# Top-k attention and a leaky-ReLU MLP on one core: other banks for the MLP's block products, later evictions in its small chunks, and four units fewer on the short path

## The chip, the cores and the metric

The kernel runs on one core of one Trainium2 chip. The metric is the device time of the whole program in microseconds; lower is better. TensorE is called PE, VectorE DVE, ScalarE ACT, GpSimd POOL and SyncE SP, as in the profile. Each of these engines works through its own queue in the order in which the program was written out, and engines wait for one another through semaphores.

## The reference

```python
# q, k, v: (8, 8, 576, 64) float32
scores = scale * np.matmul(q, k.transpose(0, 1, 3, 2))
kth = np.partition(scores, -32, axis=-1)[..., -32:-31]
scores = np.where(scores >= kth, scores, -1000000000.0)
attn = np.exp(scores - np.max(scores, axis=-1, keepdims=True))
attn = attn / (np.sum(attn, axis=-1, keepdims=True) + 1e-09)
o = np.matmul(attn, v)
x = o.transpose(0, 2, 1, 3).reshape(4608, 512)
h = x @ w_in                      # (512, 2048)
out = np.maximum(0.01 * h, h) @ w_out   # (2048, 512)
```

Each row of scores keeps its 32 largest values, the rest are set to nothing, and after the softmax and the product with `v` every token goes through a two-layer MLP.

## The kernel before, in words

**Attention in units.** Two heads form a pair; a unit is 128 rows of queries of one pair against all 576 keys, two score rows of 576 per partition. There are 144 units (32 pairs, 4.5 blocks of 128 rows each; the half blocks of two pairs share a unit). The program is a loop of steps in twos, `even(s)` and `odd(s + 1)`. In step s, DVE runs `top_k` for unit s (`cur`): it makes pairs of maxima and minima (L308), then four rounds of the eight largest (`MAX8`, L314) with replacement in between (L319). Unit s-1 (`old`) is masked and exponentiated on ACT (L329 `nleast`, L335, L338, and L343, which writes `ze`), with a bias from two small POOL instructions (L330, L331). DVE takes the reciprocal of `ze` (L347, `rz`) and ACT normalizes (L350).

In `even(s)` DVE's queue holds most of unit s's rounds, then the reciprocal for unit s-1, and only then the last round. So DVE stands still in the middle of an even step when the `ze` of unit s-1 is late. The reciprocal for unit s-2 stands after the `pairs` instructions of an even step.

**Two ways to transposed weights.** The normalized weights have to be transposed before they are multiplied with `v`. Most units go the long way: POOL splits them into 16-bit halves (`split`, L359), SP stores these to DRAM (L360) and fetches them with a DMA transpose into `wT` (L364). The units in `HASTY` go the short way: nine transposes on PE (`transpose_in_haste`, L374) and two copies on ACT (`keep_transposed`, L380). `values_at(n)` says in which step unit n's values are weighed on PE (L403, L415): two steps after the unit's odd partner if hasty, otherwise three. ACT copies the result to `x` (L426).

**The MLP in chunks.** The tokens form two small chunks of 128 tokens and 17 chunks of 256. A chunk becomes ready when the last of its values has been weighed (`attended`). The MLP is a generator that yields after every few matmuls and says how many columns it used; each step calls `mlp_steps(budget)` in seven slots, between the attention's instructions. While the small chunks are in work, the budget of one slot is `EARLY_SHARE` = 500 columns; pieces are run as long as the running debt `owed` is above zero. Afterwards `slot_budget` spreads what is left up to the next chunk.

A small chunk computes its hidden layer in four groups of 512 columns (`hidden_of_few`, L439), each evicted with the leaky ReLU by ACT (L444), turned by PE (`turned`, L455) and copied to `gT` (L456). Then 16 matmuls of 512 columns make the output (`plain`, L623), which ACT copies in two halves (L633) and sends out from its own DMA queue (L634). All these ACT instructions are issued right after the matmuls that they wait for.

A big chunk computes its hidden layer in eight groups (L536, evicted at L524) and then seven products of 256 columns (L550), since sums of blocks, made on POOL (L475), stand in for an eighth. The products live in two PSUM tiles of one bank each, `pa` and `pb`, both halved. Their evictions (`keep_sum`, L558) are put on a list, `due`, which `catch_up()` empties: it is called after every fourth matmul of a product, before the normalizing in each step, and at other set places. So an eviction of a big chunk comes into ACT's queue a little after the matmuls that it reads. Step 7 puts six sums of weights on POOL's list (`sum_weights`), which `sum_now` works off two or three at a time.

All of `mlp`'s PSUM tiles (`ph`, `pt`, `pz`) share two buffers of the pool `ps_ml`.

Of the kernel before, what the change touches and what calls it, by code (L numbers as in the profile page):

```python
# [9 lines left out]
F32 = mybir.dt.float32  # L10
# [3 lines left out]
AF = mybir.ActivationFunctionType  # L14
# [6 lines left out]
def kernel(  # L21
# [13 lines left out]
    nc = tc.nc  # L35
    NPAIR, P, S = qT.shape
# [4 lines left out]
    SLOPE = 0.01  # L41
# [21 lines left out]
    work = ctx.enter_context(tc.tile_pool(name="work", bufs=2))  # L63
    small = ctx.enter_context(tc.tile_pool(name="small", bufs=5))
    halves = ctx.enter_context(tc.tile_pool(name="halves", bufs=3, space=bass.MemoryType.DRAM))
    kept = ctx.enter_context(tc.tile_pool(name="kept", bufs=1, space=bass.MemoryType.DRAM))
# [16 lines left out]
    gT = const.tile([P, NFC, CHMAX], F32, name="gT")  # L83
# [122 lines left out]
    for b in range(B):  # L206
        first = b % 2 == 1
# [225 lines left out]
    def hidden_of_few(ch, x):  # L433

        g_of = {}
        for j in range(NFC // 4):
            ph = ps_ml.tile([P, 512], F32, name="ph", tag="ml")
            for c in range(HP):
                nc.tensor.matmul(ph, x[:, c, 0:P], w_in[c][:, j * 512:(j + 1) * 512],  # L439
                                 start=(c == 0), stop=(c == HP - 1))  # L440
                if c == 1:
                    yield 2 * 512
            g_of[j] = raws.tile([P, 2 * DMODEL], U16, name="scale", bufs=2).bitcast(F32)
            nc.scalar.activation(g_of[j], ph, AF.Prelu, alpha=SLOPE)  # L444
            yield 2 * 512
            if j:
                yield from turned(j - 1, g_of)
        few[ch] = g_of
# [3 lines left out]
    def turned(j, g_of):  # L452
        pt = ps_ml.tile([P, 4, P], F32, name="pt", tag="ml")
        for i in range(4):
            nc.tensor.transpose(pt[:, i, :], g_of[j][:, i * P:(i + 1) * P], ident)  # L455
        nc.scalar.copy(gT[:, 4 * j:4 * (j + 1), 0:P], pt)  # L456
        yield 2 * P

    HALF, COLS = NFC // 2, DMODEL // 2
    summed = {}  # L460

    def w_at(f, j):
        return w_out[f // 4][:, f % 4, j * COLS:(j + 1) * COLS]
# [38 lines left out]
    due = []  # L502

    def catch_up():
        while due:
            due.pop(0)()

    def mlp(ch):

        n = CHUNKS[ch]  # L510
        t0 = sum(CHUNKS[:ch])
        x = x_of[ch]
        if ch < EARLY:
            yield from plain(ch, n, t0, x)
            return
        if ch == EARLY:
            sum_last_weights()
        halves_of_g = gT.rearrange("p (h f) n -> p h f n", h=2)
        (g11, g21), (g12, g22) = [[halves_of_g[:, h, :, r * P:(r + 1) * P] for r in range(2)] for h in range(2)]
        s1 = raws.tile([P, HALF, P], F32, name="top", bufs=2)  # L520
        s2 = raws.tile([P, HALF, P], F32, name="top", bufs=2)

        def keep_hidden(f0, ph):
            nc.scalar.activation(halves_of_g[:, :, f0, :], ph, AF.Prelu, alpha=SLOPE)  # L524
            if f0 % 4 == 3:
                at = slice(f0 - 3, f0 + 1)
                sum_later(s1[:, at, :], g21[:, at, :], g22[:, at, :], ALU.add, name="s1")
                sum_later(s2[:, at, :], s1[:, at, :], g11[:, at, :], ALU.subtract, name="s2")
                sum_later(g21[:, at, :], g11[:, at, :], g21[:, at, :], ALU.subtract, name="g21")

        for f0 in range(HALF):
            ph = ps_ml.tile([P, 2, CHMAX], F32, name="ph", tag="ml")
            for i in range(2):
                f = f0 + i * HALF
                for c in range(HP):
                    nc.tensor.matmul(  # L536
                        ph[:, i, 0:n], w_in[c][:, f * P:(f + 1) * P], x[:, c, 0:n],
                        start=(c == 0), stop=(c == HP - 1),
                    )
                    if c == 1:  # L540
                        yield 2 * n
                if i == 0:
                    catch_up()
                    yield 2 * n
            due.append(lambda f0=f0, ph=ph: keep_hidden(f0, ph))
            yield 2 * n

        def product(to, g, w, first=False):
            for f in range(HALF):
                nc.tensor.matmul(to, g[:, f, :], w(f), start=(first and f == 0), stop=(f == HALF - 1),  # L550
                                 skip_group_check=not first)
                if f % 4 == 3:
                    catch_up()
                    yield 4 * COLS

        def keep_sum(ps):
            part = work.tile([P, COLS], F32, name="o_sb", bufs=6)
            nc.scalar.copy(part, ps)  # L558
            return part

        def place(r, j):
            return out[t0 + r * P:t0 + (r + 1) * P, j * COLS:(j + 1) * COLS]

        def of(name):
            return lambda f: summed[name][:, f, :]

        pa = ps_ml.tile([P, 512], F32, name="pz", tag="ml")
        px = pa[:, 0:COLS]
        kept_sums = {}

        def kept(name, ps, then=None):
            def keep():
                kept_sums[name] = keep_sum(ps)
                if then is not None:
                    then()
            due.append(keep)

        def add(to, other, r, j):
            part = kept_sums[to]
            sum_later(part, part, kept_sums[other], ALU.add, (place(r, j), part))  # L580

        def sum_g12():
            for f0 in (0, 4):
                at = slice(f0, f0 + 4)
                sum_later(g12[:, at, :], g12[:, at, :], s2[:, at, :], ALU.subtract, name="g12")

        yield from product(px, g11, lambda f: w_at(f, 0), first=True)
        kept("p1", px)
        pb = ps_ml.tile([P, 512], F32, name="pz", tag="ml")
        py, pd = pb[:, 0:COLS], pb[:, COLS:2 * COLS]  # L590
        pz = py
        yield from product(py, g12, lambda f: w_at(f + HALF, 0), first=True)
        sum_g12()
        kept("p2", py, lambda: add("p1", "p2", 0, 0))
        yield from product(pd, g22, of("t4"), first=True)
        kept("p4", pd)
        need("s1")
        yield from product(pz, s1, of("t1"), first=True)
        kept("p5", pz)
        need("s2")  # L600
        yield from product(px, s2, of("t2"))
        kept("u2", px)
        need("g12")
        yield from product(pz, g12, lambda f: w_at(f + HALF, 1))
        kept("p35", pz, lambda: add("u2", "p35", 0, 1))
        need("g21")
        yield from product(px, g21, lambda f: w_at(f, 1))

        def finish():
            add("p4", "u3", 1, 0)  # L610
            add("p5", "u3", 1, 1)

        kept("u3", px, finish)
        yield 0
        catch_up()
        yield 0

    def plain(ch, n, t0, x):
        yield from hidden_of_few(ch, x)
        for r0 in range(0, n, P):  # L620
            pz = ps_ml.tile([P, 512], F32, name="pz", tag="ml")
            for f in range(NFC):
                nc.tensor.matmul(  # L623
                    pz[:, 0:DMODEL], gT[:, f, r0:r0 + P], w_out[f // 4][:, f % 4, :],
                    start=(f == 0), stop=(f == NFC - 1),
                )
                if f % 2 and f + 1 < NFC:
                    yield 2 * DMODEL
                if f == 7 and ch in few:
                    yield from turned(NFC // 4 - 1, few[ch])  # L630
            for j in range(2):
                o_sb = work.tile([P, COLS], F32, name="o_sb", bufs=6)
                nc.scalar.copy(o_sb, pz[:, j * COLS:(j + 1) * COLS])  # L633
                nc.scalar.dma_start(out[t0 + r0:t0 + r0 + P, j * COLS:(j + 1) * COLS], o_sb)  # L634
            yield 2 * DMODEL

    def mlp_cost(ch):
        n = CHUNKS[ch]
# [21 lines left out]

    HASTY = (*range(8), 14, 15, 142, 143)

    def values_at(n):

# [24 lines left out]
    def slot_budget(s):  # L691

        after = [at for at, _ in ready_at if at > s]
        if len(after) >= len(CHUNKS) - EARLY:
            return EARLY_SHARE
        until = after[0] if after else s + 1
        group = [GROUP * (at % 2 == 0 and at < len(steps)) for at in range(s, until)]
        return max((backlog[0] + sum(group)) / len(group) - group[0], 0.0) / SLOTS

    EARLY_SHARE = 500  # L700
# [3 lines left out]
    with tc.manual_schedule():  # L704
# [45 lines left out]
        for n in range(len(jobs) + 1):  # L750
            if n == len(jobs) - 1:
                first = first_scores(steps[0])
# [34 lines left out]
        def keep(weighed):  # L787
            for u, po in weighed:
                keep_values(u.pairs[0], po, u.b, u.q0)
# [171 lines left out]
```

## Time and profile before

| what | value |
|---|---|
| median of 3 runs | 1468.41 us (1467.25 to 1469.81) |
| the profiled execution | 1467.3 us, span 1465.5 us, granted clock 0.978 |
| DVE busy | 1319.9 us, 90% of the span |
| PE busy | 1366.7 us, 93% |
| ACT busy | 1040.4 us, 71% |
| POOL busy | 703.3 us, 48% |
| DVE waiting for `ze` (L343) | 51.3 us, 9 times |
| PE waiting for L558's evictions of products | 18.0 us, 25 times |

All times inside the profile count from the start of the span. A row of a timeline gives the start, the length, the engine and line, the operation with what it writes and reads, and in brackets how long the engine had been idle before it and who ended that. A row of the waits gives the total in us, how often, and the longest. The second part of the page cuts the span into 40 slices of 36.6 us, with one digit for the busy tenths of each.

### The profile page before, as it was taken

The numbers are of one execution on the slowest core, as the hardware profiler recorded it, in microseconds if no ns is written. First come the engines' busy times: TensorE is split into PE (matmuls) and PEld (weight loads), VectorE is DVE, ScalarE is ACT, GpSimd is POOL, SyncE is SP. The second block draws the span as 40 slices with busy tenths as digits, with TensorE's granted clock in tenths as the row PEclk, the third lists the DMA queues.
The fourth block names the chain that finished last, engine by engine and source line by source line (L and its number), as shares of the span: only waits on it lengthen the run. The fifth ranks groups of instructions, "written<-read, shape, count | busy, mean of one in ns | idle before, by whom it ended". The sixth has DMA issues, their size and how long they took to land.

```text
span 1465.5 us, 27960 instructions
## 1 busy us (share of the span) xinstructions
PE 1366.7 (93%) x9868; PEld 1068.4 (73%) x9868; DVE 1319.9 (90%) x3401; ACT 1040.4 (71%) x2159; POOL 703.3 (48%) x788
## 2 busy tenths in 40 slices
PE   7878886989999999999999999999999999999998
PEld 2344444767887878887878887888778888878787
DVE  7986789899999999999999999999999999999600
ACT  8785677677677777777777777767677777777521
POOL 3202432554646464656564545464655555555412
PEclk9967998999999999999999999999999999999999
DMA  8950044475676546675766656665766555664400
GB/s 324 339 185 33 1 126 125 110 202 169 178 181 185 153 130 185 193 190 130 201 165 185 170 138 185 196 179 153 194 179 164 145 154 138 166 144 137 117 12 15
DMA packets 379197, 229.83 MB, mean 157 GB/s; under 512 B 316208, under 2 KB 326960, under 8 KB 377136
## 3 DMA queue, kind: packets, MB, share of 16 engines
q1 hardware_dynamic: 378480, 227.52, 55.9%
q8 instruction: 77, 1.26, 0.4%
q14 instruction: 64, 0.52, 0.1%
q10 hardware_dynamic: 576, 0.52, 0.1%
HBM read 55.77 MB, written 94.37 MB: 102 GB/s over the span
## 4 chain that ended last, share of the span: by engine, by line
DVE 69%; PE 16%; issue 7%; ACT 4%; DMA 2%; POOL 1%; ACTq 0%; DVEq 0%; POOLq 0%; SPq 0%
DVE tops L314 33%; DVE pairs L319 26%; DVE pairs L308 7%; PE ph L536 6%; PE pz L550 4%; PE wide L403 2%; DMA raw<-in_weights_dram 1%; PE pz L623 1%; PE ph L439 1%; ACT s_sb L338 1%; DVE rz L347 1%; ACT s_sb L350 1%; ACT s_sb L335 1%; ACT s_sb L244 1%; DVE w_in L156 1%
## 5 line engine op out<-in xcount | busy, mean ns | idle before, releaser
L314 DVE MAX8 tops<-pairs 128x8 f32<-128x288 f32 (+1 forms) x1152 | 636.6, 593 | 0.0
L536 PE MATMUL ph<-x,w_in 128*128 128x256 f32 x2176 | 484.1, 382 | 4.2 <-ACT gT L524 4.2
L536 PEld LDWEIGHTS ph<-x,w_in 128*128 128x128 f32 x2176 | 408.8, 190 | 84.9 <-issue 16.0
L319 DVE MATCH_REPLACE8 pairs<-tops,pairs 128x288 f32<-128x288 f32 (+1 forms) x864 | 460.9, 539 | 0.0
L359 POOL COPY split<-s_sb 128x1152 uint16<-128x1152 uint16 x264 | 294.1, 1142 | 222.3 <-ACT s_sb L350 222.3
L350 ACT ACTIVATE s_sb<-s_sb,rz 128x576 f32<-128x576 f32 x288 | 206.8, 766 | 113.5 <-DVE rz L347 113.1
L330 POOL TENSOR_TENSOR nbias<-tops 128x2 f32<-128x2 f32 x144 | 73.1, 507 | 424.2 <-DVE tops L314 404.6
L550 PE MATMUL pz<-w_out,gT 128*128 128x256 f32 x1088 | 241.3, 379 | 1.7 <-ACT gT L524 1.7
L550 PEld LDWEIGHTS pz<-w_out,gT 128*128 128x128 f32 x1088 | 206.4, 190 | 31.1 <-ACT gT L524 2.5
L308 DVE TENSOR_TENSOR pairs<-s_sb 128x576 f32<-128x576 f32 x288 | 216.4, 791 | 9.9 <-ACT nleast L329 0.5
L338 ACT ACTIVATE s_sb<-s_sb,nbias 128x576 f32<-128x576 f32 x288 | 223.2, 781 | 0.8 <-POOL nbias L331 0.8
L335 ACT ACTIVATE s_sb<-s_sb,nleast 128x576 f32<-128x576 f32 x288 | 207.7, 768 | 4.8
L403 PE MATMUL wide<-wT,vt 128*64 128x128 f32 (+1 forms) x2560 | 157.4, 287 | 16.2 <-ACT wT L380 13.7
L403 PEld LDWEIGHTS wide<-wT,vt 128*64 128x64 f32 (+1 forms) x2560 | 129.9, 140 | 49.3 <-issue 30.4
L550 PE MATMUL pz<-raw,top 128*128 128x256 f32 x544 | 125.9, 384 | 8.4 <-ACT o_sb L558 5.7
L524 ACT ACTIVATE gT<-ph 128x512 f32<-128x512 f32 x136 | 80.6, 593 | 64.3 <-PE ph L536 64.2
L550 PEld LDWEIGHTS pz<-raw,top 128*128 128x128 f32 x544 | 100.9, 190 | 32.8 <-issue 13.0
L558 ACT COPY o_sb<-pz 128x256 f32<-128x256 f32 x119 | 44.6, 375 | 102.9 <-PE pz L550 93.6
L235 PE MATMUL wide<-kt,qt 64*64 64x352 f32 x1040 | 104.6, 474 | 0.0
L244 ACT COPY s_sb<-wide 128x704 f32<-128x704 f32 x130 | 99.4, 764 | 0.3 <-PE wide L235 0.3
L331 POOL TENSOR_SCALAR nbias<-nbias 128x2 f32<-128x2 f32 x144 | 84.0, 583 | 12.6
L550 PE MATMUL pz<-raw,gT 128*128 128x256 f32 x272 | 66.0, 385 | 12.9 <-ACT o_sb L558 12.3
(81 smaller groups left out, 1202.5 us busy)
## 6 DMA issues: line engine op xcount, KB each, us to landing
apart<-split SPq DMA_DIRECT2D x264, 288.0 KB, 2.3
raw<-in_weights_dram SPq DMA_DIRECT2D x15, 1024.0 KB, 7.0
vt<-in_vk_dram SPq DMA_DIRECT2D x32, 320.0 KB, 3.8
qt<-in_qT_dram SPq DMA_DIRECT2D x32, 288.0 KB, 3.7
kt<-in_kT_dram SPq DMA_DIRECT2D x32, 288.0 KB, 3.7
out_dram<-o_sb SPq DMA_DIRECT2D x68, 128.0 KB, 2.2
kept<-gT SPq DMA_DIRECT2D x12, 576.0 KB, 3.8
s_sb<-kept SPq DMA_DIRECT2D x12, 576.0 KB, 4.8
```

The source lines that it names most:

```text
L235: nc.tensor.matmul(to[r0:r0 + LEFT, i, :], qt[d, q0:q0 + LEFT], kt[d, k0:k1], start=True, stop=True)
L244: nc.scalar.copy(u.both[:, :, k0:k1], to)
L308: nc.vector.tensor_tensor(pairs[:, :, n, :], u.both[:, :, 0:HS], u.both[:, :, HS:S], op)
L314: nc.vector.max(out=u.tops[:, i, r, :], in_=rest[i])
L319: nc.vector.match_replace(out=rest[i], in_to_replace=u.tops[:, i, r, :], in_values=rest[i], imm_value=LOWEST)
L335: nc.scalar.activation(u.s[i], u.s[i], AF.Prelu, bias=u.nleast[:, i:i + 1], scale=1.0, alpha=BELOW)
L338: nc.scalar.activation(u.s[i], u.s[i], AF.Exp, bias=u.nbias[:, i:i + 1], scale=SCALE, accum_out=u.z[:, i:i + 1])
L350: nc.scalar.activation(u.s[i], u.s[i], AF.Copy, bias=0.0, scale=u.rz[:, i:i + 1])
L359: nc.gpsimd.tensor_copy(split, pairs[:, :, h])
L403: nc.tensor.matmul(po[n * D:(n + 1) * D, side, 0:P], v_of[u.pairs[0]][k, at, side, :], u.wT[k, at + side * NKC if at + 1 < NKC else at, :] ...
L536: nc.tensor.matmul(ph[:, i, 0:n], w_in[c][:, f * P:(f + 1) * P], x[:, c, 0:n], start=(c == 0), stop=(c == HP - 1),)
L550: nc.tensor.matmul(to, g[:, f, :], w(f), start=(first and f == 0), stop=(f == HALF - 1), skip_group_check=not first)
```

## The change

It has four parts. In big chunks the order of the first products changes from p1, p2, p4 to p4, p2, p1, so that successive products alternate between `pa` and `pb`. In small chunks the evictions of the hidden groups, of the turned groups and of the result go through `due`, and `catch_up()` is called half a group later. In the steps whose older unit is hasty, `EARLY_SHARE` is multiplied by 0.6. Units 4 to 7 leave `HASTY`, so their weights go the long way, their values are weighed in steps 8 and 10, and the second small chunk becomes ready in step 11.

```diff
     def hidden_of_few(ch, x):
+        def keep(j, ph):
+            nc.scalar.activation(g_of[j], ph, AF.Prelu, alpha=SLOPE)
+
...
                 if c == 1:
+                    catch_up()
                     yield 2 * 512
             g_of[j] = raws.tile([P, 2 * DMODEL], U16, name="scale", bufs=2).bitcast(F32)
-            nc.scalar.activation(g_of[j], ph, AF.Prelu, alpha=SLOPE)
+            due.append(lambda j=j, ph=ph: keep(j, ph))
             yield 2 * 512
...
     def turned(j, g_of):
-        nc.scalar.copy(gT[:, 4 * j:4 * (j + 1), 0:P], pt)
+        catch_up()
+        due.append(lambda: nc.scalar.copy(gT[:, 4 * j:4 * (j + 1), 0:P], pt))
...
-        px = pa[:, 0:COLS]
+        px, pd = pa[:, 0:COLS], pa[:, COLS:2 * COLS]
...
-        yield from product(px, g11, lambda f: w_at(f, 0), first=True)
-        kept("p1", px)
+        yield from product(pd, g22, of("t4"), first=True)
+        kept("p4", pd)
         pb = ps_ml.tile([P, 512], F32, name="pz", tag="ml")
-        py, pd = pb[:, 0:COLS], pb[:, COLS:2 * COLS]
-        pz = py
+        py, pz = pb[:, 0:COLS], pb[:, COLS:2 * COLS]
         yield from product(py, g12, lambda f: w_at(f + HALF, 0), first=True)
         sum_g12()
-        kept("p2", py, lambda: add("p1", "p2", 0, 0))
-        yield from product(pd, g22, of("t4"), first=True)
-        kept("p4", pd)
+        kept("p2", py)
+        yield from product(px, g11, lambda f: w_at(f, 0), first=True)
+        kept("p1", px, lambda: add("p1", "p2", 0, 0))
...
+    def send_off(pz, t):
+        for j in range(2):
+            o_sb = work.tile([P, COLS], F32, name="o_sb", bufs=6)
+            nc.scalar.copy(o_sb, pz[:, j * COLS:(j + 1) * COLS])
+            nc.scalar.dma_start(out[t:t + P, j * COLS:(j + 1) * COLS], o_sb)
+
     def plain(ch, n, t0, x):
...
                 if f % 2 and f + 1 < NFC:
+                    catch_up()
                     yield 2 * DMODEL
...
-            for j in range(2):
-                o_sb = work.tile([P, COLS], F32, name="o_sb", bufs=6)
-                nc.scalar.copy(o_sb, pz[:, j * COLS:(j + 1) * COLS])
-                nc.scalar.dma_start(out[t0 + r0:t0 + r0 + P, j * COLS:(j + 1) * COLS], o_sb)
+            due.append(lambda: send_off(pz, t0 + r0))
             yield 2 * DMODEL
+            catch_up()
...
-    HASTY = (*range(8), 14, 15, 142, 143)
+    HASTY = (*range(4), 14, 15, 142, 143)
...
         if len(after) >= len(CHUNKS) - EARLY:
-            return EARLY_SHARE
+            return EARLY_SHARE * (0.6 if s - 2 in HASTY else 1.0)
```

## The prediction

> **What bounds the kernel now.** I read the page first: which engine is full, and whose chain ends last.
>
> ```profile
> PE 1366.7 (93%) x9868; PEld 1068.4 (73%) x9868; DVE 1319.9 (90%) x3401; ACT 1040.4 (71%) x2159; POOL 703.3 (48%) x788
> ...
> DVE  7986789899999999999999999999999999999600
> ...
> DVE 69%; PE 16%; issue 7%; ACT 4%; DMA 2%; POOL 1%; ACTq 0%; DVEq 0%; POOLq 0%; SPq 0%
> ```
>
> VectorE (DVE) is the chain, full from slice 8 on; its holes lie in slices 3 to 7 and at the end. TensorE (PE) is nearly as full, so a gain on DVE counts only if PE can follow. Second, who DVE waits for, and where (DVE's waits and timeline):
>
> ```profile
> DVE rz L347 <- ACT ze L343: 51.3, 9, 11.1
> ```
>
> ```profile
> 110.47 0.17 DVE L347 RECIPROCAL rz<-ze 128x2 f32<-128x2 f32 x1 [6.56 <-ACT ze L343]
> ...
> 140.10 0.17 DVE L347 RECIPROCAL rz<-ze 128x2 f32<-128x2 f32 x1 [11.13 <-ACT ze L343]
> ...
> 163.61 0.17 DVE L347 RECIPROCAL rz<-ze 128x2 f32<-128x2 f32 x1 [4.89 <-ACT ze L343]
> ...
> 190.14 0.17 DVE L347 RECIPROCAL rz<-ze 128x2 f32<-128x2 f32 x1 [8.82 <-ACT ze L343]
> ```
>
> Step s is the one in which DVE searches unit s. Counting the L308 rows, these four are steps 4, 6, 8 and 10; step 8 has a 0.80 besides, step 6 a 0.68, step 18 a 5.31, and the last two steps 3.66 and 9.44: the 51.3. Between 266 and 1368 us DVE never waits for more than 0.5 us, so what its start gains is carried to about unit 141. Third, why `ze` is late: ScalarE (ACT) takes its queue in order.
>
> ```profile
> 131.39 0.60 ACT L444 ACTIVATE scale<-ph 128x512 f32<-128x512 f32 x1 [3.83 <-PE ph L439]
> 134.82 0.60 ACT L444 ACTIVATE scale<-ph 128x512 f32<-128x512 f32 x1 [2.84 <-PE ph L439]
> 135.31 0.20 ACT L329 ACTIVATE nleast<-tops 128x2 f32<-128x2 f32 x1
> ...
> 182.39 0.37 ACT L633 COPY o_sb<-pz 128x256 f32<-128x256 f32 x1 [4.92 <-PE pz L623]
> ...
> 183.62 1.68 ACTq L634 DMA_DIRECT2D out_dram<-o_sb  x1
> 185.34 0.20 ACT L329 ACTIVATE nleast<-tops 128x2 f32<-128x2 f32 x1 [1.76 <-issue]
> ```
>
> Unit 5's `tops` were ready at 120.8, yet `nleast` started at 135.31, behind two evictions that wait for TensorE. In step 10 it stood behind the result's eviction and its DMA issue. Last, PE's rows in the tail, where DVE is done:
>
> ```profile
> 1444.34 1.99 PE L550 MATMUL pz<-raw,gT 128*128 128x256 f32 x8 [0.52 <-ACT o_sb L558]
> ...
> 1448.61 5.42 PE L550 MATMUL pz<-raw,top 128*128 128x256 f32 x24 [0.55 <-ACT o_sb L558]
> ```
>
> Both stalls are in the middle of a product: it shares its bank with the one just finished, whose eviction is queued after the new product's first four matmuls.
>
> **Step 6, less MLP and late evictions.** Nothing changes before the `x` copy at 127.18. The share of 300 instead of 500 puts 3 pieces (6 matmuls) into step 5 instead of 4, and only the first group's eviction now stands ahead of `nleast`; the second comes after `ze`. The first ends at 131.9 as now, so `nleast` moves from 135.31 to 131.9: **3.4 us**. ACT's work after it is the same (4.8 us to `ze`), so the wait falls from 11.13 to about 7.7. It does not vanish: `x` waits for the weighing matmuls (3.27 us) and the eviction for four matmuls (3.83 us), and both stay. The 6.56 in step 4 stays too: no MLP is in it.
>
> **Steps 7 to 9, units 4 to 7 by POOL and DMA.** For four units the 9 transposes on PE (1.15 to 1.87 us a unit here, 6.0 in all) and the two `wT` copies on ACT (1.16 a unit) go. Each unit costs two `split` copies on POOL (2.23) and two stores and a DMA transpose on SP. SP's queue holds nothing else between 118 and 190 us, so no load waits behind them. From normalized weights to weighing this route takes about 2.2 + 2.3 (store) + 2.7 (issue) + 4.7 (landing) = 12 us, and values are now weighed in steps 8 and 10, not 7 and 9. I walked the new queues on from the `ze` at 136.6 with the durations of these rows. DVE: step 7 begins at 138.2 (the last two searches of step 6 take 1.4), step 8 at 147.0 (8.8 a step). ACT for unit 6: one eviction and one gT copy, normalizing to 139.0, masks to 140.5, an eviction to 141.3, score copies to 143.6 (PE's scores run from 140.7 to 142.8), exponentials with a gT copy between them to 145.7, `ze` at 146, needed at 148. For unit 7: an eviction to 147.5 (its matmuls run from 143.4 to 147.0), gT copy, masks to 149.8, normalizing of unit 6 from 150.6, exponentials to 153.6, `ze` at 153.8, needed at 156. For unit 8: 164.4, needed at 169. The 0.80 and 4.89 of step 8 go: **5.7 us**. What is late next is the third group's eviction, which still stands between masks and exponentials, but its matmuls end at about 140.7, as ACT gets there.
>
> **Step 10.** The result's eviction moves behind `ze` of the same step, and chunk 1 starts at step 11. The whole 8.82 goes. Its cover is the end of step 10: the two copies and issues (3 us) stand before the normalizing of unit 9, which has a step to spare; without that cover up to 3 us return. Sum of the three places: 3.4 + 5.7 + 8.8 = **17.9 us**.
>
> **What comes back: DVE against POOL.** The six weight sums on POOL (2.35 each) now start behind two splits, and DVE arrives earlier. DVE's `pairs` step has two SBUF inputs:
>
> ```profile
> 267.66 4.77 DVE L308 TENSOR_TENSOR pairs<-s_sb 128x576 f32<-128x576 f32 x2
> ```
>
> It takes 1.43 alone; beside two POOL sums it took 4.77 (+3.3), and 1.96 (+0.5) where a sum was just ending (1155.35). Now the sums of steps 7 to 9 miss all three `pairs`. In my walk sums run at 142.0 to 149.0 and 154.3 to 159.0, with `pairs` of units 8 and 9 due at 147.0 and 157.9. Bounds: 0 to 2 x 3.3 us. In the 4.77 row the sums end at 271.78 and DVE goes on at 272.36, so I take what is left of the running sum: 2.0 (149.0 less 147.0) + 1.1 (159.0 less 157.9) = **3.1 us back**. The Trainium skill ("SBUF — State Buffer", section "Who interferes with whom") speaks against the change here: the port pair that the two engines share is an exclusive lock, so that a VectorE instruction with two SBUF inputs waits for the whole of a running GpSimd instruction that reads SBUF. By that rule the early gain would be 14.8 before the next charge; by the mildest row, 0.5 a step, it would be 16.9. A further 0.5 I charge to steps 12 to 14, where chunk 1's third group waits for an eviction behind a normalizing and scores of unit 14 come about 1 us before need (bounds 0 and 3). Early net: 17.9 - 3.1 - 0.5 = **14.3 us**. Step 18 I leave at 5.31: its weighing took 3.87 us at 251.4, against 2.35 at full clock, after PE had idled (granted clock 0.88 from 190 to 260); chunk 1's last matmuls now lie closer to it, which I leave to the range as 0 to 1.5 us.
>
> **The steady part: 0.** DVE's pace stays. PE loses stalls of 0.5 to 0.6 twice a chunk (18.0 us for `pz <- o_sb` in all), but these hide under DVE. PE then needs 70.0 busy us of every 71.1 (window 1121.72 to 1192.84), so it keeps up with the earlier DVE. Its order after step 17 is the same but for the products.
>
> **The tail.** From 1321 us the chain is PE. Last chunk: 0.52 + 0.55; the one before (at 1381.60 and 1385.87): 0.46 + 0.55. Together 2.1 us, on the path. PE also enters the tail ahead by some of what it no longer stalls; scores come 6.4 to 10.8 us before need throughout, so ACT, paced by DVE, seems to hold it. Bounds 0 and 6 us (DVE's last waits, 3.66 and 9.44, are for evictions behind PE); I take 1.5. After the last product nothing changes (copy, POOL add, 2.2 us store). Tail: **3.6 us**.
>
> **Sum.** 14.3 + 3.6 = 17.9. The profiled execution took 1467.3 (span 1465.5), the median of the three runs is 1468.41, 1.1 more: 1467.3 - 17.9 + 1.1 = **1450.5**.
>
> **Rivals.** (a) *Waits only move.* The late evictions come up at the next step's front and hold `nleast` there; steps 8 and 10 keep half of their 14.5 us of waits (7.3), and the sums collide fully (6.6, not 3.1). Total 17.9 - 10.8 = 7.1: about 1461. For it: 0.5 to 1.5 us margins in my walk. Against: two of the three evictions ahead of `nleast` would find their matmuls done.
>
> (b) *Slower: POOL's sums hit DVE's `pairs` in every chunk.* PE, freed of stalls, delivers gT earlier, POOL sums earlier, and in each of the 17 big chunks two `pairs` steps fall under a 1.27 us sum, costing 0.9 to 1.06 each as at 942.87 (2.33) and 1297.58 (2.51), against about 0.3 a chunk now. 1.4 a chunk more is 24 us: 1450.5 + 24 = 1474. It decides from 1.05 a chunk (17.9 over 17). Against: the sums stand behind splits in POOL's queue, and splits wait for DVE's reciprocals through ACT (222.3 us of POOL's waiting), so their phase is DVE's own.
>
> (c) *More.* No collisions, step 18 shorter by 1.5, the tail by 6 more: 17.9 + 1.5 + 8.1 = 27.5: 1441.
>
> **How the numbers follow.** Forecast 0.62, (a) 0.18, (b) 0.10, (c) 0.10. Faster by over 0.2% (2.9 us, about what a measurement of this kernel can tell from no change) holds in the forecast, in (c) and in most of (a): 0.87. Within 0.2%: 0.04, between (a) and (b). Slower 0.09. The range 1439 to 1462.5 takes in the forecast's bounds (collisions 0 to 6.6, tail 2.1 to 8.1), (c) and (a), and leaves out (b) and what fails beyond (a).
>
> **What would show it.** DVE's waits for `ze`: 51.3 falls to about 33, or less by what the tail sheds; in step 6 about 7.7, none in steps 8 and 10, 6.56 still in step 4. Unit 20's `pairs`, now at 279.8, starts near 265. `pairs` of units 8 and 9 take 2.5 to 3.5 us. The two mid-product stalls of the last chunk are gone. Wrong if waits of over 2 us stand in steps 7 to 16, if many `pairs` rows after 300 us exceed 1.9, or if PE waits for scores' buffers.

## The result, and the profile after

The changed kernel takes 1447.8 us (median of 4 runs, 1447.51 to 1450.17) against 1467.88 us for the kernel before (4 runs in the same comparison): a ratio of 0.9865, 95% interval 0.9847 to 0.9882, 20.1 us less. The forecast was 1450.5. The profiled execution took 1447.51 us, its span is 1445.7 against 1465.5. Line numbers move: L439, L444, L550, L558, L623 and L633 of before are L443, L438, L556, L564, L634 and L626 here, POOL's sums L475 are L481.

The page of the changed kernel, busy times, DVE's forty slices and the chain that ended last:

```profile
PE 1363.7 (94%) x9830; PEld 1066.7 (74%) x9832; DVE 1318.6 (91%) x3401; ACT 1028.6 (71%) x2151; POOL 712.5 (49%) x796
...
DVE  7987998999999999999999999999999999999700
...
DVE 69%; PE 18%; issue 7%; ACT 4%; DMA 1%; POOL 1%; DVEq 0%; POOLq 0%; SPq 0%
```

DVE's share of the chain is what it was, its busy time too (1318.6 against 1319.9): what went is waiting. Its waits for `ze`, and its timeline:

```profile
DVE rz L347 <- ACT ze L343: 35.0, 8, 8.0
```

```profile
134.73 0.17 DVE L347 RECIPROCAL rz<-ze 128x2 f32<-128x2 f32 x1 [6.12 <-ACT ze L343]
...
145.03 3.39 DVE L308 TENSOR_TENSOR pairs<-s_sb 128x576 f32<-128x576 f32 x2
155.83 3.32 DVE L308 TENSOR_TENSOR pairs<-s_sb 128x576 f32<-128x576 f32 x2
...
204.55 0.17 DVE L347 RECIPROCAL rz<-ze 128x2 f32<-128x2 f32 x1 [1.31 <-ACT ze L343]
...
230.31 0.17 DVE L347 RECIPROCAL rz<-ze 128x2 f32<-128x2 f32 x1 [2.03 <-ACT ze L343]
...
256.09 0.17 DVE L347 RECIPROCAL rz<-ze 128x2 f32<-128x2 f32 x1 [8.03 <-ACT ze L343]
```

The waits of steps 8 and 10 are gone, that of step 6 is 6.12 for 11.13, and that of step 4 stays (6.74 for 6.56). Two stretched `pairs` (units 8 and 9) are new, and so are the waits in steps 14 and 16; step 18 rose from 5.31 to 8.03. The start of `pairs` by unit shows where the time went:

| stretch | before | after | gain |
|---|---|---|---|
| unit 0 starts | 61.25 | 60.56 | 0.7 (ahead of anything changed) |
| unit 0 to 11 | 130.41 | 114.81 | 15.6 |
| unit 11 to 20 | 88.13 | 94.36 | -6.2 |
| unit 20 to 141 | 1071.94 | 1067.22 | 4.7 |
| unit 141 to the end | 113.8 | 108.8 | 5.0 |

The sum is 19.8, the difference of the spans. In the last 30 us PE's products now run through; the two stalls that the prediction quoted are not there:

```profile
1416.65 3.62 PE L556 MATMUL pz<-raw,gT 128*128 128x256 f32 x16
1420.10 7.07 PE L556 MATMUL pz<-w_out,gT 128*128 128x256 f32 x32
1427.01 7.07 PE L556 MATMUL pz<-raw,top 128*128 128x256 f32 x32
```

### The profile page after: what moved, and what is told of

It reads as the page before. It is cut to its first block, busy times and chain, and to the rows that moved or that the text cites. A ratio compares the mean times of both kernels' runs of the same rounds, so it can differ in the third digit from the quotient of the medians.

```text
span 1445.7 us, 27893 instructions
## 1 busy us (share of the span) xinstructions
PE 1363.7 (94%) x9830; PEld 1066.7 (74%) x9832; DVE 1318.6 (91%) x3401; ACT 1028.6 (71%) x2151; POOL 712.5 (49%) x796
## 4 chain that ended last, share of the span: by engine, by line
DVE 69%; PE 18%; issue 7%; ACT 4%; DMA 1%; POOL 1%; DVEq 0%; POOLq 0%; SPq 0%
DVE tops L314 33%; DVE pairs L319 25%; DVE pairs L308 7%; PE ph L542 6%; PE pz L556 6%; PE wide L403 3%; ACT s_sb L338 1%; DVE rz L347 1%; ACT s_sb L350 1%; PE wide L235 1%; DMA raw<-in_weights_dram 1%; PE wide L288 1%; DVE w_out L156 1%; ACT s_sb L244 1%; DVE scale L153 1%
## 5 line engine op out<-in xcount | busy, mean ns | idle before, releaser
L359 POOL COPY split<-s_sb 128x1152 uint16<-128x1152 uint16 x272 | 303.0, 1142 | 191.0 <-ACT s_sb L350 190.6
L350 ACT ACTIVATE s_sb<-s_sb,rz 128x576 f32<-128x576 f32 x288 | 206.9, 766 | 151.7 <-DVE rz L347 151.7
L556 PE MATMUL pz<-w_out,gT 128*128 128x256 f32 x1088 | 241.0, 379 | 2.2 <-ACT o_sb L564 1.7
L556 PEld LDWEIGHTS pz<-w_out,gT 128*128 128x128 f32 x1088 | 206.3, 190 | 31.9 <-POOL nbias L331 2.1
L335 ACT ACTIVATE s_sb<-s_sb,nleast 128x576 f32<-128x576 f32 x288 | 207.6, 768 | 4.7
L556 PE MATMUL pz<-raw,top 128*128 128x256 f32 x544 | 124.4, 383 | 3.0 <-ACT o_sb L564 3.0
L556 PEld LDWEIGHTS pz<-raw,top 128*128 128x128 f32 x544 | 101.3, 190 | 26.0 <-issue 7.0
L329 ACT ACTIVATE nleast<-tops 128x2 f32<-128x2 f32 x144 | 28.6, 199 | 91.7 <-DVE tops L314 90.5
L564 ACT COPY o_sb<-pz 128x256 f32<-128x256 f32 x119 | 44.5, 374 | 65.2 <-PE pz L556 63.6
```

The costliest lines, as they stand in the source:

```text
L335: nc.scalar.activation(u.s[i], u.s[i], AF.Prelu, bias=u.nleast[:, i:i + 1], scale=1.0, alpha=BELOW)
L350: nc.scalar.activation(u.s[i], u.s[i], AF.Copy, bias=0.0, scale=u.rz[:, i:i + 1])
L359: nc.gpsimd.tensor_copy(split, pairs[:, :, h])
```

## The experiments

Ten kernels ran in three comparisons, each with its own runs of the kernel before (nine in a comparison). "Gain" below is that median of before less the kernel's. Unit 20's `pairs`, counted from unit 0's, sums up the early part of the profiled execution.

| kernel | us | before | ratio (95%) | gain | unit 0 to 20 |
|---|---|---|---|---|---|
| before | | | | | 218.5 |
| the change | 1447.80 | 1467.88 | 0.9865 (0.9847 to 0.9882) | 20.1 | 209.2 |
| e1: before, banks | 1455.89 | 1466.98 | 0.9925 (0.9913 to 0.9938) | 11.1 | 217.2 |
| e2: change, old banks | 1457.35 | 1466.98 | 0.9938 (0.9926 to 0.9951) | 9.6 | 209.0 |
| e3: change, 4 to 7 hasty | 1448.80 | 1466.98 | 0.9877 (0.9861 to 0.9892) | 18.2 | 210.2 |
| e4: change, share 500 | 1449.12 | 1466.03 | 0.9882 (0.9869 to 0.9896) | 16.9 | 211.1 |
| e5: change, evictions at once | 1442.34 | 1466.98 | 0.9834 (0.9821 to 0.9847) | 24.6 | 203.0 |
| e6: change, POOL's sums in odd steps | 1443.52 | 1466.03 | 0.9848 (0.9834 to 0.9862) | 22.5 | 203.2 |
| e8: before, banks, 4 to 7 long way | 1446.31 | 1466.03 | 0.9866 (0.9852 to 0.9879) | 19.7 | 207.6 |
| e9: e5 with e6 | 1440.94 | 1466.03 | 0.9829 (0.9816 to 0.9842) | 25.1 | 202.8 |
| e10: e9, chunk 1 sooner | 1444.78 | 1467.21 | 0.9845 (0.9832 to 0.9859) | 22.4 | 208.0 |
| e11: e9, less of chunk 2 | 1438.61 | 1467.21 | 0.9799 (0.9786 to 0.9812) | 28.6 | 198.8 |

The medians alone do not tell every pair of kernels apart. The intervals of the change and of e3, e4 and e6 overlap, and so do those of e5 and e9, of e6 and e9, and of e9 and e10; that of e5 touches the change's. Between such kernels the reading rests on the rows of one trace each.

**e1, the product order alone**, put into the kernel before:

```diff
-        px = pa[:, 0:COLS]
+        px, pd = pa[:, 0:COLS], pa[:, COLS:2 * COLS]
...
-        yield from product(px, g11, lambda f: w_at(f, 0), first=True)
-        kept("p1", px)
+        yield from product(pd, g22, of("t4"), first=True)
+        kept("p4", pd)
         pb = ps_ml.tile([P, 512], F32, name="pz", tag="ml")
-        py, pd = pb[:, 0:COLS], pb[:, COLS:2 * COLS]
-        pz = py
+        py, pz = pb[:, 0:COLS], pb[:, COLS:2 * COLS]
...
-        yield from product(pd, g22, of("t4"), first=True)
-        kept("p4", pd)
+        yield from product(px, g11, lambda f: w_at(f, 0), first=True)
+        kept("p1", px, lambda: add("p1", "p2", 0, 0))
```

> The kernel before with the new order of the block products alone (p4, p2, p1), nothing else. Theory A (the bank order lets TensorE run ahead of VectorE, so ScalarE no longer waits for it, POOL's splits and sums end before VectorE's pairs instruction, and the tail is shorter): some 9 to 10 us faster than before, about 1458 us; no pairs row above 1.9 us between 300 and 1340 us; unit 20's pairs still start near 279.8 us; unit 141's some 4 to 5 us earlier than 1351.7. Theory B (the steady part gained because the start shifted all phases, the banks give only the 2.1 us of stalls at the end): about 1465.5 us, and pairs rows of 1.9 to 2.5 us are still there.

Measured: 11.1 us of gain. By its profile 1.4 lie ahead of unit 20, where no big chunk's product has run yet, so they are scatter; units 20 to 141 take 1067.9 (before 1071.9) and the tail 108.6 (before 113.8). The banks are worth about 9 us, 4 of them in the steady part that the prediction put at nothing. One stretched `pairs` row is left between 300 and 1340 us (1.99 us at 322.06), where theory A had none above 1.9; before has seven.

**e2, the change without the new order** (the same lines turned back).

> The changed kernel with the old order of the block products. Theory A: 9 to 10 us slower than the changed kernel, about 1457.5 us, the pairs rows of 1.9 to 2.5 us between 300 and 1340 us are back, and the start (unit 20's pairs at 269.7) is unchanged. Theory B: about 1450 us, no such rows.

Measured: 9.6 of gain, 10.5 less than the change. Units 20 to 141 take 1072.1 and the tail 114.0, as before, and eight stretched `pairs` rows (1.65 to 2.51 us) are back between 430 and 1300 us. Together with e1 this settles that the order alone makes both parts.

What the order does there is read from the rows. ACT, POOL and then DVE at unit 119, first before:

```profile
1149.21 0.60 ACT L524 ACTIVATE gT<-ph 128x512 f32<-128x512 f32 x1 [1.11 <-PE ph L536]
1149.70 1.43 ACT L350 ACTIVATE s_sb<-s_sb,rz 128x576 f32<-128x576 f32 x2
```

```profile
1154.74 1.28 POOL L475 TENSOR_TENSOR top<-top,gT 128x512 f32<-128x512 f32 x1
```

```profile
1155.35 1.96 DVE L308 TENSOR_TENSOR pairs<-s_sb 128x576 f32<-128x576 f32 x2
```

and after:

```profile
1135.53 0.57 ACT L530 ACTIVATE gT<-ph 128x512 f32<-128x512 f32 x1
1136.01 1.43 ACT L350 ACTIVATE s_sb<-s_sb,rz 128x576 f32<-128x576 f32 x2
```

```profile
1141.04 1.28 POOL L481 TENSOR_TENSOR top<-top,gT 128x512 f32<-128x512 f32 x1
```

```profile
1142.88 1.43 DVE L308 TENSOR_TENSOR pairs<-s_sb 128x576 f32<-128x576 f32 x2
```

Before, the sum still runs when `pairs` begins (1154.74 + 1.28 = 1156.02); after, it has ended at 1142.32. Before has seven rows of `pairs` over 1.6 us between 300 and 1340 us; what they take over 1.43 is 4.3 in sum. After has none. That is most of the 4.7.

Why POOL comes earlier stands in ACT's rows. The reciprocal that the normalizing (L350) needs starts at 1147.86 before and at 1135.39 after. Before, the normalizing follows 1.84 us later, behind an eviction of a hidden group that waited 1.11 us for PE; after, 0.62 later, behind one that waited for nothing. The split and the sums behind it come earlier by as much. All seven stretched rows of before have this shape: the normalizing follows the reciprocal after 1.52 to 2.59 us, behind such an eviction with a wait of 0.79 to 1.29. At the same seven units it follows after 0.61 or 0.62 in the changed kernel and in e1, and `pairs` takes 1.43. ACT's waits from 300 to 1310 us, before and after, say the same of the whole stretch:

```profile
ACT s_sb L350 <- DVE rz L347: 103.2, 57, 2.5
ACT o_sb L558 <- PE pz L550: 60.9, 46, 3.1
...
ACT gT L524 <- PE ph L536: 29.6, 39, 1.5
```

```profile
ACT s_sb L350 <- DVE rz L347: 136.1, 57, 2.7
...
ACT o_sb L564 <- PE pz L556: 36.1, 21, 3.1
ACT gT L530 <- PE ph L542: 1.8, 3, 1.2
```

ACT's evictions wait less for PE (90.5 us in these two lines before, 37.9 after), the hidden groups' hardly at all, and ACT waits longer for `rz` instead (136.1 for 103.2).

**e3, units 4 to 7 hasty again**, the smaller share kept where the change has it:

```diff
-    HASTY = (*range(4), 14, 15, 142, 143)
+    HASTY = (*range(8), 14, 15, 142, 143)
+    HURRIED = (*range(4), 14, 15, 142, 143)
...
-            return EARLY_SHARE * (0.6 if s - 2 in HASTY else 1.0)
+            return EARLY_SHARE * (0.6 if s - 2 in HURRIED else 1.0)
```

> The changed kernel with units 4 to 7 on the short path again (the smaller share stays where it is in the changed kernel). Theory A (late evictions and the smaller share make most of the early gain; the long way for units 4 to 7 brings the two collisions of pairs with the weight sums, 3.9 us, and pushes chunk 1 into steps 15 to 18, 6 us): within 3 us of 1447.8, either way; pairs of units 8 and 9 take 1.5 us again, waits in steps 8 or 10 come back by 2 to 5 us, and step 18 waits 5.3 us rather than 8.0. Theory B (the short path's waits in ScalarE's queue were the main cost): 6 us slower or more, waits of over 3 us each in steps 8 and 10.

Measured: 1.9 us less gain than the change. Without the long way the waits of steps 8, 10 and 12 are 7.20, 2.18 and 1.86, but no `pairs` collides and step 18 waits 4.87, not 8.03. On the short way step 10 does wait less with the late evictions (9.05 in e1, 2.18 here), though the smaller share ahead of it differs too, and step 8 waits more (7.20 for 0.64 and 4.89).

**e5, the small chunks' evictions at once**, as before, all else as changed:

```diff
-            due.append(lambda j=j, ph=ph: keep(j, ph))
+            nc.scalar.activation(g_of[j], ph, AF.Prelu, alpha=SLOPE)
...
-        catch_up()
-        due.append(lambda: nc.scalar.copy(gT[:, 4 * j:4 * (j + 1), 0:P], pt))
+        nc.scalar.copy(gT[:, 4 * j:4 * (j + 1), 0:P], pt)
...
-            due.append(lambda: send_off(pz, t0 + r0))
+            for j in range(2):
+                o_sb = work.tile([P, COLS], F32, name="o_sb", bufs=6)
+                nc.scalar.copy(o_sb, pz[:, j * COLS:(j + 1) * COLS])
...
```

> The changed kernel with the small chunks' evictions issued at once again, as before the change. Theory A (these evictions, standing in ScalarE's queue ahead of the mask and the exponentials, made ze late): 6 to 10 us slower, about 1455 to 1458 us, with a wait of some 5 to 9 us in step 10, where the result's copies and their DMA issues stand, and waits in step 8. Theory B (the smaller share and the long way for units 4 to 7 did it alone): within 2 us of 1447.8.

Measured: 4.5 us more gain. Both theories missed: the late evictions are a loss. Steps 8, 10, 14 and 16 have no wait at all, step 18 has 5.57. The changed kernel's PE rows show what they cost:

```profile
186.29 3.70 PE L443 MATMUL ph<-w_in,x 128*128 128x512 f32 x8 [1.51 <-ACT scale L438]
...
193.66 3.30 PE L443 MATMUL ph<-w_in,x 128*128 128x512 f32 x4 [3.16 <-ACT scale L438]
...
205.05 7.13 PE L634 MATMUL pz<-w_out,gT 128*128 128x512 f32 x16 [1.20 <-ACT scale L438]
```

With two buffers in `ps_ml`, the next group's first matmul waits for an eviction that now stands further back in ACT's queue: behind a mask whose `nleast` waits for DVE (2.36 us at 184.08), behind a normalizing that waits for DVE (1.90 us at 191.69), and behind exponentials and `ze` (to 204.51). PE's waits on `scale` between 125 and 260 us are 8.0 in the change (6.6 for `ph`, 1.4 for `pz`); here they are 3.0, with 1.4 more on a copy to `gT`. Chunk 1 falls behind, and its x, scores and evictions reach ACT late in steps 14 to 18.

**e4, share 500 everywhere:**

```diff
-            return EARLY_SHARE * (0.6 if s - 2 in HASTY else 1.0)
+            return EARLY_SHARE
```

> The changed kernel with the full share of 500 columns a slot in the hurried steps too (late evictions and the long way for units 4 to 7 stay). Theory A (the smaller share takes one group's eviction out of ScalarE's queue ahead of unit 5's mask and exponentials): step 6 waits 8 to 9.5 us instead of 6.1, the rest moves little: 1.5 to 3.5 us slower, 1449.5 to 1451. Theory B (the share is idle, late evictions alone do it): within 1 us of 1447.8.

Measured: 3.2 us less gain. Step 6 waits 10.68. Some of that comes back: the `pairs` of units 8 and 9 take 3.38 and 2.50 instead of 3.39 and 3.32, and step 14 has no wait.

**e8, banks and the long way only:** e1 with one line.

```diff
-    HASTY = (*range(8), 14, 15, 142, 143)
+    HASTY = (*range(4), 14, 15, 142, 143)
```

> The kernel before with the new order of the block products and units 4 to 7 on the long way, nothing else (evictions at once, full share). Theory A (the long way takes the waits of the x copies and of keep_transposed out of the odd steps and so carries the gain of steps 8 and 10; the share carries step 6): step 6 waits 9.5 to 11 us, none in steps 8 and 10: 2.5 to 4 us slower than the 1442.3 of the kernel with evictions at once. Theory B (the long way gains only together with the smaller share): waits of over 3 us in steps 8 or 10, 1450 us or more.

Measured: 8.6 us more gain than e1. Step 6 waits 11.13, as before, and steps 8 and 10 not at all, with every eviction issued at once and the full share. So the long way alone carries both. The result's copy still stands ahead of unit 9's `nleast` and does no harm: its matmuls have ended, and `nleast` waits for DVE's `tops` after it. ACT's rows in e8:

```profile
167.26 0.35 ACT L632 COPY o_sb<-pz 128x256 f32<-128x256 f32 x1
...
170.81 0.21 ACT L329 ACTIVATE nleast<-tops 128x2 f32<-128x2 f32 x1 [2.37 <-DVE tops L314]
```

From e8 to e5 only the share differs: 4.9 us more gain, and a step 6 of 7.69 for 11.13. The other wait that is shorter in e5 is that of step 4 (4.88 for 6.86), where no MLP runs: it is not the share's.

**e6, POOL's weight sums moved** out of the even steps, the rest as changed:

```diff
-            sum_now(2)
+            sum_now(0 if s < 14 else 2)
...
-            sum_now(3)
+            sum_now(2 if s < 14 else 3)
```

> The changed kernel with the six weight sums spread over steps 7, 9 and 11, two in each, none in even steps (before step 14). Theory A (VectorE's pairs wait for the running POOL sum): pairs of units 8 and 9 fall from 3.39 and 3.32 us to about 1.45, nothing comes back: 3.9 us faster, about 1444 us. Theory B (the stretched rows only fill time that the next ze would have taken): a wait for ze of 1 to 2 us appears in step 8 or 10 instead, 1446 to 1448 us.

Measured: 2.4 us more gain. No `pairs` row is stretched before unit 19, so the collisions of units 8 and 9 were those six sums. Unit 20 is 6.0 us earlier, more than the 3.9 that the two rows lost: step 14 does not wait either, and the wait that theory B put in step 8 or 10 does not come up.

**e9, both mends** (the edits of e5 and e6).

> Both: small chunks' evictions at once, and the weight sums two at a time in steps 7, 9 and 11. Theory A (the two costs lie in different steps, so they add): 1442.3 less 3.9, about 1438.4 us. Theory B (with evictions at once the stretched pairs hide a late ze): 1440 us or more, and a wait in step 8 or 10.

Measured: 0.5 us more gain than e5. The mends do not add up, as theory B said, but not in its place (step 8 waits 0.77, step 10 not at all): unit 14 comes 2.0 us earlier than in e5 (139.0 and 141.1 after unit 0), unit 19 at the same time (190.7 and 190.9), since step 18's wait grew from 5.57 to 7.42. Something other than DVE sets `ze` there. ACT's rows ahead of it:

```profile
242.41 0.60 ACT L524 ACTIVATE gT<-ph 128x512 f32<-128x512 f32 x1 [3.91 <-PE ph L536]
242.91 0.20 ACT L329 ACTIVATE nleast<-tops 128x2 f32<-128x2 f32 x1
```

It is the picture of step 6 again: unit 17's `nleast` stands behind an eviction that waits for a big chunk's first matmuls.

**e10, chunk 1 finished sooner**, on e9:

```diff
-            return EARLY_SHARE * (0.6 if s - 2 in HASTY else 1.0)
+            return EARLY_SHARE * (0.5 if s - 2 in HASTY else 1.0)
...
-    EARLY_SHARE = 500
+    EARLY_SHARE = 600
```

> Built on the kernel with evictions at once and POOL's weight sums in odd steps (median 1440.94 us), whose earlier DVE was eaten by a wait of 7.42 us in step 18. Share 600 instead of 500 outside the hurried steps, 300 in them as before, so the second small chunk's product ends sooner. Theory A: the chain into step 18 starts at ACT's copy of that product, 216.90 us after 2.27 us of waiting, ahead of unit 15's nleast at 218.49. The wait for the product goes, nleast of unit 15 and what hangs on it (the normalizing of unit 14, the transposes, the weighing, x) move up by 1.5 to 2.3 us; step 18's wait falls to about 5.5; median 1438.6 to 1439.5. Rival B: the chain into step 18 hangs on chunk 2's first evictions and on PE at its lower clock after idling; PE, done with the product sooner, only idles longer. Step 18's wait stays over 7; median 1440.5 to 1441.5, the same within 0.1%.

Measured: 2.7 us less gain than e9. Both theories missed, as neither looked at steps 8 to 10: with more matmuls ahead of them the waits there return (1.93 and 2.92), and the copy that was to come sooner still waits for its product (2.85 us at 217.05).

**e11, less of chunk 2 in step 17**, on e9:

```diff
-        return max((backlog[0] + sum(group)) / len(group) - group[0], 0.0) / SLOTS
+        return max((backlog[0] + sum(group)) / len(group) - group[0], 0.0) / SLOTS * (0.6 if s - 2 in HASTY and s < 20 else 1.0)
```

> The same base (median 1440.94 us). In step 17, whose older unit is hasty, the budget of the first big chunk is multiplied by 0.6, so that its first hidden group is evicted after unit 17's nleast and mask instead of ahead of them, and the second after ze. Theory A: unit 17's ze hangs on these two evictions (ACT waits of 3.91 and 1.29 us for their matmuls): nleast goes from 242.91 to about 239.5, the first eviction still ends at 243.0 as its matmuls set it, and ze moves from 249.34 to about 246.5. Step 18's wait falls from 7.42 to about 4.6; median about 1438.1. Rival B: PE, which needs 70 of every 71 us in the steady part, starts that much behind and gives it back in the first chunks or in the tail: step 18's wait falls but the median stays within 1 us of 1440.9.

Measured: 3.5 us more gain than e9, the fastest kernel of this study: 28.6 us under before, 8.5 more than the change. The `nleast` row now precedes the eviction, and step 18 waits 4.10:

```profile
237.73 0.21 ACT L329 ACTIVATE nleast<-tops 128x2 f32<-128x2 f32 x1
...
241.86 0.60 ACT L524 ACTIVATE gT<-ph 128x512 f32<-128x512 f32 x1 [2.45 <-PE ph L536]
```

## Why the prediction was right, and where it was not

The total, 1450.5 against 1447.8, is nearer than its terms: the early part gave 9.4 where 14.3 were written, the steady part and the tail 9.7 where 3.6 were. That the total came so near is luck: 4.9 too little and 6.1 too much almost cancel.

**Step 6: right.** 3.4 was written for one eviction fewer ahead of `nleast`. The wait fell by 5.0. ACT's rows in the changed kernel show the step as it was worked out:

```profile
129.45 0.60 ACT L438 ACTIVATE scale<-ph 128x512 f32<-128x512 f32 x1 [3.20 <-PE ph L443]
129.95 0.20 ACT L329 ACTIVATE nleast<-tops 128x2 f32<-128x2 f32 x1
...
134.60 0.58 ACT L438 ACTIVATE scale<-ph 128x512 f32<-128x512 f32 x1
```

The share does it. The eight kernels with the smaller share wait 6.12 to 8.99 in step 6, 7.2 in the mean; the four with the full one (before, e1, e4, e8) 9.56 to 11.13, 10.6 in the mean: 3.4 less, as written. The late evictions, named beside it, show no part in it: four of the eight have them (6.8 in the mean) and four have not (7.6), e4 has them with the full share and waits 10.68. The 1.6 beyond what was written are within the scatter of single traces: e2 has the same instructions up to there and waits 8.99.

**Steps 7 to 9: right.** 5.7 were written; the waits of step 8 (0.80 and 4.89) are gone, and e8 shows that the long way does it.

**Step 10: the number right, the reason wrong.** All of 8.82 went, but the result's eviction need not move behind `ze` for that: e8 leaves it ahead of unit 9's `nleast`. By then the product had ended, and chunk 1 begins a step later, the second half of what was written. On the short way the written reason may hold (e3, 2.18 in place of 9.05 in e1).

**What comes back: right, and a little small.** 3.1 was written. The two rows lost 1.96 and 1.89, 3.9, and e6 took both away by moving the sums. The price was read rightly, as what is left of the running sum: the sums under the two rows end at 147.13 and 157.87 us, 2.10 and 2.04 after `pairs` started. The Trainium skill ("SBUF — State Buffer", section "Who interferes with whom") calls the shared port pair an exclusive lock held for a whole instruction; rows of 3.39 and 3.32 us against 1.43 alone agree with it.

**Steps 12 to 18: the step that failed.** The prediction put 0.5 on chunk 1's third group, with 3 as the bound, and left step 18 at 5.31. Unit 20 started at 269.7 us, not near 265. From unit 11 to 20 the change lost 6.2: waits of 1.31 and 2.03 in steps 14 and 16, and 2.72 more in step 18. It had seen one group of matmuls wait for an eviction behind a normalizing, and priced it at 0.5. With two buffers PE waits in that way three times (1.51, 3.16 and 1.20 us), and ACT and DVE then wait for PE. In e5, without late evictions, unit 11 to 20 takes 88.4, as before. The price is not fixed, though: with the sums moved as well, e6 (late) and e9 (at once) reach unit 20 within 0.4 us of each other, since step 18 then waits for PE and ACT in both. Their medians differ by 2.6, with intervals that overlap, so how much of it remains there is open.

**The steady part: wrong.** "DVE's pace stays" took DVE's search for a fixed length. The prediction itself counted 0.3 us a chunk of stretched `pairs`, as the ground for rival (b), and asked only whether it could rise. With the new order it fell to next to none (no row in the change, one in e1, eight again in e2): 4.7 instead of 0. Rival (b) had the mechanism, POOL's sums against `pairs`, with the wrong sign. The argument against it, that sums stand behind splits and splits wait for reciprocals through ACT, names the true chain; what was missed is that ACT, held up by evictions that waited for PE, came late in it before.

**The tail: right in kind, 5.0 for 3.6.** The last chunk's two stalls (1.07) are gone. DVE's last two waits, 3.66 and 9.44 before, are

```profile
1355.04 0.17 DVE L347 RECIPROCAL rz<-ze 128x2 f32<-128x2 f32 x1 [1.88 <-ACT ze L343]
...
1374.57 0.17 DVE L347 RECIPROCAL rz<-ze 128x2 f32<-128x2 f32 x1 [8.03 <-ACT ze L343]
```

3.2 less: PE's lead and the stalls of the chunk before the last together, for which 1.5 and 1.0 were written. The 0.7 that is left of the 5.0 was not traced further, but for 0.2 in unit 141's `pairs` (1.66 before, 1.43 after).

**The rivals.** (a) had late evictions come up at the next steps' fronts, and put 7.3 of its 10.8 us on steps 8 and 10; they cost about 6, in steps 14 to 18. "Waits of over 2 us in steps 7 to 16" was named as a sign against the forecast: the 2.03 in step 16 just is one, and it marked the term that failed.

## What to carry to other kernels

Delaying an eviction so that a more urgent instruction goes first pays only as long as its buffer is not the next thing that TensorE needs: count the buffers, and look at what the instruction that it is put behind waits for. Fewer matmuls ahead of the urgent instruction did the same for it at no such price, in step 6 and again in step 17 (e11). A stall that hides under the bottleneck may still set the phase of a third engine, so before a steady part is put at nothing, look through the bottleneck's own rows for lengths that vary.

## What the runs showed of the hardware

PE is slower after some gaps, and single traces of the early part differ by it. In the changed kernel the 40 weighing matmuls of one unit take 2.35 us at 214.27, straight after other matmuls, but 4.18 us at 231.23:

```profile
227.91 2.00 PE L374 MATMUL wide<-ident,s_sb 128*128 128x128 f32 x9 [4.00 <-ACT s_sb L350]
231.23 4.18 PE L403 MATMUL wide<-wT,vt 128*64 128x128 f32 x40 [1.32 <-ACT wT L380]
```

PE had idled for 4.00 and 1.32 us ahead of them, and the granted clock is 0.78 between 220 and 235 us, 1.00 between 200 and 220. So DVE's wait in step 18 contains part of a slow weighing. The Trainium skill says ("TensorE: Matmul & The Clock Gate", section "What's actually happening") that about 3.4 us of idling halve the clock, in windows that run freely, so that the same kernel can meet them at another phase. The gap of 4.00 us and the rows after it fit that.

Kernels with the same program up to step 6 waited 6.12 (the change) and 8.99 (e2) there, behind weighing that kept `x` waiting 2.32 and 4.30 us. The 40 matmuls took 2.35 us in the one and 4.32 in the other, after gaps of 2.32 and 2.33, both under 3.4: the length of the last gap does not decide it, and what does is not shown here. A difference of 2 us in one wait between two single traces is therefore weak evidence, unless other traces or the medians go with it.
